# A decode step of attention and a small feed-forward: wo loaded as 24 and 8 rows a partition, and O placed by four matmuls

## The chip, the cores and the metric

The kernel runs on one core of one Trainium2 chip. The metric is the device time of one execution in microseconds (us): 343.64 us before the change, the median of three runs (343.55 to 343.87).

## The reference

One token for each of two sequences goes through attention over a cache of 4096 keys (32 heads of 128) and through a feed-forward layer with ReLU, and a sigmoid gate mixes the two. Cut to what matters:

```python
g = sigmoid((x * gate_w).sum(-1, keepdims=True))          # x: [2, 1, 512]
q = (x @ wq).reshape(2, 1, 32, 128).transpose(0, 2, 1, 3)
p = softmax(einsum("bhqd,bhkd->bhqk", q, k_cache) * 128 ** -0.5)
o = einsum("bhqk,bhkd->bhqd", p, v_cache)
a = o.transpose(0, 2, 1, 3).reshape(2, 1, 4096) @ wo       # wo: [4096, 512]
b = relu(x @ w1) @ w2                                      # w1: [512, 1376], w2: [1376, 512]
out = g * a + (1 - g) * b
```

All inputs are bf16. K and V are 67 MB each, wo is 4 MB, w2 1.4 MB; with wq and w1 145 MB are read once.

## The kernel before

**Memory.** K and V are cut into 8 units each (32,768 rows, 64 KB a partition). One tile `kv` of three regions (128 partitions x 3 x 64 KB) takes the units in turn, in an order written out by hand (`order`, line 164): K units 0 to 4, then V and K in turn, then V units 3 to 7. All transfers are issued by SP, in program order, and each waits only for PE to have finished with the unit that held its region three places earlier (`freed`). The last V unit comes in two transfers (48 rows of 64, then 16). Behind it, in the region that V unit 5 leaves, come w2 and wo.

**How the work is staged.** For a K unit DVE turns both halves in place (line 337), and PE accumulates scores for it (lines 342 and 370). After four K units the softmax of one sequence runs on DVE and ACT, and POOL spreads the probabilities into the weights `ptm` (line 408). For a V unit PE does 64 matmuls (line 425); ACT copies the sums out, POOL masks them, and a matmul gathers them (line 445). For the last V unit DVE does the masking (line 436).

**The tail.** After the last V unit PE's program order is: a few steps of w2 (`project_first`, lines 485 to 489: the rows of w2 in its first, small transfers), the gather of V unit 7, the other steps of w2's first part, `o_place`, then `project`. DVE scales O into `O_sb` (lines 459 and 461; 32 partitions, one for each head). `o_place` (line 465) brings O from heads on partitions to the layout in which it multiplies wo: 16 matmuls with shifted slices of a selection matrix `srow` (made once by POOL at line 253), into a PSUM area of 128 x 64, which ACT copies to `oW` (line 474). `project` (line 491) is 32 steps over wo and 9 over w2; one `step` (line 479) is two matmuls of 256 columns, side by side in two column groups of the array, for one row of wo or w2 a partition. A step that needs a new transfer waits for that transfer's semaphore, and everything behind it on PE waits too. At the end DVE and ACT cast the two halves of the sum (lines 502 and 504), and SP stores the output (line 244).

**The layout of wo and w2.** wo's 4096 rows lie as two halves of 2048; a partition holds 16 successive rows of each half. The three transfers are the first half (16 rows a partition, 16 KB), then 12 and 4 rows of the second (12 KB and 4 KB). `project` waits for them at steps 0, 16 and 28 (`lands`, line 492). w2's first 224 rows come in five small transfers ahead of wo; the other 1152 rows follow wo in blocks of 3, 3, 2 and 1 rows a partition (`W2`, line 210: semaphore, first row, rows a partition, first index). The hidden layer (`ffn_h`, line 308) is computed at the start, in the layout that w2's blocks ask for: for a block of n rows a partition, its weight loads take every n-th column of w1.

## Time and profile before

| | |
|---|---|
| median of three runs | 343.64 us |
| the profiled execution | 343.64 us |
| its span (first to last instruction) | 342.3 us |
| mean granted TensorE clock | 0.83 |
| PE busy | 190.9 us (56%) |
| DVE busy | 155.4 us (45%) |
| transfers of K, V and weights: share of the 16 DMA engines' time | 98.6% |
| read from HBM | 145.43 MB, 425 GB/s over the span |

The rows of a profile read as follows. A group or a timeline row names the engine, the line of the kernel, the operation, and what it writes and reads (`PS<-kv,oW` writes PSUM from the tiles kv and oW), with shape and count; in brackets stands how long the engine was idle ahead of it, and what ended that. PE is TensorE's matmuls, PEld its weight loads, which overlap matmuls. The chain of waits starts at the last instruction and goes back, at each step to what released it. The windows view gives, for chosen stretches, how long each engine was busy and, in brackets, how many instructions ran; PEclk is the clock that TensorE was granted, as a share of full speed. The granted clock is 1.00 or 0.50 in this kernel. A matmul's duration is longer than the distance to the next one, since they are pipelined.

### The profile page before, as it was taken

What the parts mean: (1) busy time and instruction counts of PE and PEld (TensorE: products, weight loads), DVE (VectorE), ACT (ScalarE), POOL (GpSimd) and SP (SyncE); (2) the same over time, 40 slices, a digit from 0 to 9 for tenths busy, and PEclk for the clock granted to TensorE, in tenths of its full rate; (3) what the DMA queues carried; (4) which work ended last, traced back from release to release, by engine and by line L of the source; (5) the groups of instructions that cost most, each with busy time, mean ns of one, the idle gap of its engine ahead of it and who ended that gap; (6) DMA issues with size and microseconds to landing.
All of it is one profiled execution on the core that took longest, in us unless ns stands there. A gap on an engine that the chain in (4) does not pass through costs nothing.

```text
span 342.3 us, 2418 instructions
## 1 busy us (share of the span) xinstructions
PE 190.9 (56%) x1294; PEld 40.1 (12%) x910; DVE 155.4 (45%) x41; ACT 13.1 (4%) x31; POOL 43.2 (13%) x55
## 2 busy tenths in 40 slices
PE   0520069595988909850992059900995532407386
PEld 0220001010000100010111001200012201102133
DVE  1000697979889779309900594009916000000010
ACT  1010000000000020000000000000003000000000
POOL 2000000000000004032005000050003250502300
PEclk9999999898798976995898559975799585857688
DMA  8998989899998989899999999898999999999996
GB/s 322 456 484 375 482 375 482 383 475 414 438 475 383 490 368 490 375 477 391 467 398 454 437 421 482 375 484 383 475 406 452 406 446 421 437 440 421 389 426 253
DMA packets 3810, 145.56 MB, mean 425 GB/s; under 512 B 445, under 2 KB 582, under 8 KB 1094
## 3 DMA queue, kind: packets, MB, share of 16 engines
q1 hardware_dynamic: 3796, 145.43, 98.6%
q8 instruction: 8, 0.13, 0.2%
q10 hardware_dynamic: 6, 0.00, 0.0%
HBM read 145.43 MB, written 0.00 MB: 425 GB/s over the span
## 4 chain that ended last, share of the span: by engine, by line
DMA 65%; PE 22%; DVE 10%; SPq 2%; issue 0%
DMA kv<-in_A_k_cache_dram 44%; PE PS L342 14%; DMA kv<-in_B_w_dram 11%; DVE kv L337 10%; DMA kv<-in_A_v_cache_dram 10%; PE PS L370 5%; PE PS L425 3%; SPq L231 1%; SPq L241 1%; SPq L236 0%; PE PS L481 0%; PE PS L445 0%; SPq L234 0%; SPq L216 0%; DVE ptm L502 0%
## 5 line engine op out<-in xcount | busy, mean ns | idle before, releaser
L337 DVE STREAM_TRANSPOSE kv<-kv 128x8192 uint32<-128x8192 uint32 x16 | 138.5, 8690 | 83.7 <-DMA kv<-in_A_k_cache_dram 83.7
L342 PE MATMUL PS<-kv,zero 128*128 128x512 bf16 x384 | 117.4, 417 | 0.0
L370 PE MATMUL PS<-kv,zero 128*128 128x512 bf16 x128 | 54.0, 422 | 93.8 <-DVE kv L337 84.6
L425 PE MATMUL PS<-kv,ptm 128*32 128x512 bf16 x512 | 39.4, 452 | 33.5 <-DMA kv<-in_A_v_cache_dram 33.5
L370 PEld LDWEIGHTS PS<-kv,zero 128*128 128x128 bf16 x128 | 13.3, 104 | 207.6 <-issue 112.3
L408 POOL TENSOR_TENSOR ptm<-E,mask 128x512 bf16<-128x512 bf16 x32 | 32.2, 1039 | 12.0 <-DVE E L399 11.1
L436 DVE TENSOR_TENSOR X<-PS,maskc 128x512 f32<-128x512 f32 x1 | 0.7, 692 | 62.7 <-PE PS L425 62.7
L425 PEld LDWEIGHTS PS<-kv,ptm 128*32 128x32 bf16 x512 | 16.1, 110 | 57.6 <-issue 48.2
L440 POOL TENSOR_TENSOR X<-X,maskc 128x512 f32<-128x512 f32 x7 | 7.3, 1038 | 114.3 <-ACT X L439 114.3
L330 POOL TENSOR_TENSOR zero<-q_sb,mask 128x32 bf16<-128x32 bf16 x8 | 2.0, 252 | 149.1 <-PE PS L342 133.6
L445 PE MATMUL PS<-X,zero 128*32 128x512 f32 x16 | 8.4, 604 | 6.8 <-POOL X L440 6.6
L439 ACT ACTIVATE X<-PS 128x512 f32<-128x512 f32 x7 | 4.2, 597 | 142.9 <-PE PS L425 142.9
L376 DVE TENSOR_REDUCE zero<-PS 128x2 f32<-128x2048 f32 x2 | 4.5, 2272 | 7.8 <-PE PS L342 7.8
L399 DVE STREAM_TRANSPOSE E<-E 128x2048 bf16<-128x2048 bf16 x2 | 4.6, 2311 | 4.7 <-ACT E L391 4.7
L294 PE MATMUL PS<-kv,zero 128*32 128x512 bf16 x32 | 3.6, 630 | 4.1 <-DMA kv<-in_A_wq_dram 4.1
L383 ACT ACTIVATE nrow<-mmax 128x32 f32<-128x32 f32 x2 | 0.5, 229 | 141.4 <-DVE mmax L380 141.4
L481 PE MATMUL PS<-kv,oW 128*2 128x256 bf16 x64 | 5.5, 344 | 0.7 <-DMA kv<-in_A_wo_dram 0.7
L272 PE MATMUL PS<-kv 3*128 3x3 bf16 x4 | 0.3, 166 | 8.1 <-DMA kv<-in_gate_w_dram 8.1
L502 DVE CAST ptm<-PS 2x256 bf16<-2x256 f32 x1 | 0.4, 412 | 9.3 <-PE PS L481 9.3
L301 DVE STREAM_TRANSPOSE ptm<-PS 128x1024 f32<-128x1024 f32 x1 | 1.2, 1249 | 7.2 <-PE PS L294 7.2
L391 ACT ACTIVATE E<-PS,negm 128x1024 bf16<-128x1024 f32 x4 | 4.4, 1110 | 0.6 <-DVE negm L387 0.6
L481 PE MATMUL PS<-kv,hT 20*2 20x256 bf16 (+2 forms) x42 | 3.2, 269 | 1.0 <-DMA kv<-in_B_w_dram 0.8
(43 smaller groups left out, 28.1 us busy)
## 6 DMA issues: line engine op xcount, KB each, us to landing
kv<-in_A_v_cache_dram SPq DMA_DIRECT2D x1, 6144.0 KB, 46.8
kv<-in_A_wq_dram SPq DMA_DIRECT2D x1, 4096.0 KB, 12.1
kv<-in_A_v_cache_dram SPq DMA_DIRECT2D x1, 2048.0 KB, 51.4
kv<-in_A_wo_dram SPq DMA_DIRECT2D x1, 2048.0 KB, 35.2
kv<-in_A_wo_dram SPq DMA_DIRECT2D x1, 1536.0 KB, 38.4
kv<-in_B_w_dram SPq DMA_DIRECT2D x1, 1376.0 KB, 15.0
kv<-in_B_w_dram SPq DMA_DIRECT2D x2, 384.0 KB, 40.0
kv<-in_A_wo_dram SPq DMA_DIRECT2D x1, 512.0 KB, 39.2
```

The costliest lines, as they stand in the source:

```text
L337: dve(lambda v, h=h: v.transpose(out=reg[:, 8192 * h:8192 * (h + 1)], in_=reg[:, 8192 * h:8192 * (h + 1)]), dwaits=([landed(what)] if h == ...
L342: return e.add_instruction(mybir.InstMatmult(name=nc.get_next_instruction_name(), engine=mybir.EngineType.PE, ins=[e.lower_ap(rhs), e.lowe ...
L370: return e.matmul(dst, lhsT=w, rhs=m, start=first, stop=final, skip_group_check=True)
L376: dve(lambda v: v.tensor_reduce(out=mpad[:, 0:2], in_=PSF[:, 0:2048].rearrange("p (x h q) -> p h x q", h=2, q=16), axis=AX.XY, op=ALU.max) ...
L391: act(lambda a, h=h: a.activation(out=E[:].rearrange("p (x h q) -> p h x q", h=2, q=16)[:, h], in_=PSF[:, 0:2048].rearrange("p (x h q) -> ...
L399: dve(lambda v: v.transpose(out=E[:], in_=E[:]), waits=[f"act_exp{b}"], signal=f"dve_et{b}")
L408: pool(lambda g, src=src, dst=dst: g.tensor_tensor(out=dst, in0=src, in1=msk, op=ALU.mult), waits=(([f"dve_et{b}"] if ub == 0 else []) + ( ...
L425: pe(lambda e, ci=ci, t=t: e.matmul(psf(32 * t, 32 * t + 32, c0, 512), lhsT=ptm[:, ci].rearrange("p c h -> p (c h)"), rhs=rows[:, 512 * ci ...
L439: act(lambda e: e.activation(out=X2[:], in_=src, func=ACT.Copy), waits=[f"pe_v_{v}"], signal=f"act_x_{v}")
L440: pool(lambda e: e.tensor_tensor(out=X, in0=X, in1=msk, op=ALU.mult), waits=[f"act_x_{v}"] + ([] if v else ["dve_setup"]), signal=f"pool_x ...
L445: pe(lambda e: e.matmul(psf(0, 32, O_C0, 512), lhsT=selx[:, 24 - 8 * ub:56 - 8 * ub], rhs=X2[:], start=(ub == 0), stop=(ub == 3), skip_gro ...
L481: pe(lambda e, g=g: e.matmul(psf(64 * g, 64 * g + 2, FIN_C0, 256), lhsT=w, rhs=m[:, 256 * g:256 * g + 256], start=start, stop=stop, tile_p ...
```

## The change

wo is laid out as 32 successive rows a partition and loaded in two transfers, of 24 and of 8 rows (24 KB and 8 KB a partition); `project` waits at steps 0 and 24. The order of wo's rows over partitions changes, and with it the placing of O: partition p now needs rows 32p to 32p + 31, a quarter of one head, so four matmuls of 64 columns do it, with one row of selection for each quarter, and `srow` shrinks from 263 to 131 columns. w2's two blocks of 3 rows become one of 6. The order of the steps on PE and of the transfers on SP stays as it was, and so do the bytes; two transfers and two semaphores go.

```diff
-    srow = zero[0:32, 788:920].bitcast(bf16)[:, 0:263]
+    srow = zero[0:32, 788:854].bitcast(bf16)[:, 0:131]
...
-    W2 = (("w2p", 0, 11, 0), ("w2p", 220, 1, 11), ("w2a", 224, 3, 12), ("w2b", 608, 3, 15), ("w2c", 992, 2, 18), ("w2d", 1248, 1, 20))
+    W2 = (("w2p", 0, 11, 0), ("w2p", 220, 1, 11), ("w2a", 224, 6, 12), ("w2c", 992, 2, 18), ("w2d", 1248, 1, 20))
...
-    for i, (x, r0, r1) in enumerate(((0, 0, 16), (1, 0, 12), (1, 12, 16))):
-        sp(lambda e, i=i, x=x, r0=r0, r1=r1: e.dma_start(
-            wo_sb[:, x * 8192 + r0 * 512:x * 8192 + r1 * 512],
-            A_wo[x * 2048:(x + 1) * 2048, :].rearrange("(p r) n -> p (r n)", p=128)[:, r0 * 512:r1 * 512])
+    for i, (a, b) in enumerate(((0, 24), (24, 32))):
+        sp(lambda e, i=i, a=a, b=b: e.dma_start(wo_sb[:, a * 512:b * 512], A_wo.rearrange("(p r) n -> p (r n)", r=32)[:, a * 512:b * 512])
            .then_inc(sem[f"wo{i}"], 16))
...
-        pool(lambda g: g.affine_select(out=srow, in_=srow, pattern=[[-1, 263]], compare_op=ALU.not_equal, fill=1.0,
-                                       base=7, channel_multiplier=8), waits=["c_zero"], signal="c_srow")
+        pool(lambda g: g.affine_select(out=srow, in_=srow, pattern=[[-1, 131]], compare_op=ALU.not_equal, fill=1.0,
+                                       base=3, channel_multiplier=4), waits=["c_zero"], signal="c_srow")
...
     def o_place():
-        for x in range(2):
-            for dq in range(8):
-                s0 = 128 * x - dq + 7
-                pe(lambda e, x=x, dq=dq, s0=s0: e.matmul(psf(0, 128, R_C0 + 32 * x, 32), lhsT=srow[:, s0:s0 + 128],
-                                                         rhs=O_sb[:, :, 16 * dq:16 * dq + 16], start=(dq == 0), stop=(dq == 7),
-                                                         tile_position=(0, 0), skip_group_check=True),
...
-        act(lambda a: a.activation(out=oW[:].rearrange("p (x r) c -> p x r c", x=2),
-                                   in_=psf(0, 128, R_C0, 64).rearrange("p (x b r) -> p x r b", x=2, b=2), func=ACT.Copy),
+        for dq in range(4):
+            pe(lambda e, dq=dq: e.matmul(psf(0, 128, R_C0, 64), lhsT=srow[:, 3 - dq:131 - dq],
+                                         rhs=O_sb[:, :, 32 * dq:32 * dq + 32], start=(dq == 0), stop=(dq == 3),
+                                         tile_position=(0, 0), skip_group_check=True),
+               waits=(["dve_O0", "dve_O1", "c_srow"] if dq == 0 else []), signal=("pe_R" if dq == 3 else None))
+        act(lambda a: a.activation(out=oW[:], in_=psf(0, 128, R_C0, 64).rearrange("p (b r) -> p r b", b=2), func=ACT.Copy),
             waits=["pe_R"], signal="act_oW")
...
     def project():
-        lands = {0: "wo0", 16: "wo1", 28: "wo2"}
+        lands = {0: "wo0", 24: "wo1"}
```

## The prediction

> **What bounds the kernel now.** I read the chain of waits first, then the timeline of the last 12 us, then the windows view with stretches cut where the granted clock changes. Until 327 us the page shows the DMA engines at 8 to 9 tenths in every slice, and the change touches nothing there that anybody waits for. What counts is the tail. The chain of waits ends so:

> ```profile
> 300.88 39.17 DMA kv<-in_B_w_dram
> 340.10 0.58 PE PS L481 x6
> 340.70 0.41 DVE ptm L502
> ```

> Columns: start, duration, what. The last w2 transfers land, six matmuls follow, then the cast. The end is set by a landing, and PE stands ready for it. The timeline shows how PE got there:

> ```profile
> 330.25 0.92 PE L481 MATMUL PS<-kv,hT 20*2 20x256 bf16 x14
> 331.47 0.56 PE L469 MATMUL PS<-zero 32*128 32x32 bf16 x16 [0.29 <-DVE zero L461]
> 332.07 0.22 ACT L474 ACTIVATE oW<-PS 128x64 bf16<-128x64 f32 x1 [17.67 <-PE PS L469]
> 332.69 5.47 PE L481 MATMUL PS<-kv,oW 128*2 128x256 bf16 x64 [0.66 <-DMA kv<-in_A_wo_dram]
> 336.24 1.62 PEld L481 LDWEIGHTS PS<-kv,oW 128*2 128x2 bf16 x32 [0.48 <-DMA kv<-in_A_wo_dram]
> 338.51 0.20 PEld L481 LDWEIGHTS PS<-kv,hT 128*2 128x2 bf16 x6 [0.65 <-DMA kv<-in_B_w_dram]
> 339.47 0.20 PEld L481 LDWEIGHTS PS<-kv,hT 128*2 128x2 bf16 x6 [0.76 <-DMA kv<-in_B_w_dram]
> 340.10 0.09 PEld L481 LDWEIGHTS PS<-kv,hT 128*2 128x2 bf16 x4 [0.43 <-DMA kv<-in_B_w_dram]
> 340.38 0.08 PEld L481 LDWEIGHTS PS<-kv,hT 128*2 128x2 bf16 x2 [0.20 <-DMA kv<-in_B_w_dram]
> 340.70 0.41 DVE L502 CAST ptm<-PS 2x256 bf16<-2x256 f32 x1 [9.29 <-PE PS L481]
> ```

> Each PEld row is PE released by a landing: the second wo transfer at 336.24, then w2a, w2b, w2c and w2d at 338.51, 339.47, 340.10 and 340.38. The first wo transfer released PE at 332.69. So a **step** (one row of wo or w2, two matmuls) is done while the next rows land.

> The third thing is the clock. In these rows the columns are the stretch, its length, PE busy (instructions), the other four engines, PEclk, DMA share, GB/s:

> ```profile
> 127.90:131.31 3.41, 2.46 (x6) 0.25 (x2) 2.57 (x2) 0.81 (x2) 0.18 (x1) 0.50 0.84 365
> 288.33:291.74 3.41, 2.99 (x32) 1.32 (x36) 0.00 (x0) 0.00 (x0) 0.00 (x0) 0.50 1.15 500
> 291.74:295.15 3.41, 2.10 (x40) 0.89 (x32) 0.00 (x0) 0.60 (x1) 0.58 (x1) 1.00 0.75 327
> 315.63:319.05 3.42, 0.98 (x2) 0.07 (x2) 0.00 (x0) 0.00 (x0) 3.42 (x4) 1.00 1.06 460
> 329.29:332.70 3.41, 2.46 (x34) 1.12 (x36) 1.01 (x2) 0.22 (x1) 0.00 (x0) 1.00 0.99 412
> 332.70:336.11 3.41, 3.41 (x32) 1.90 (x32) 0.00 (x0) 0.00 (x0) 0.00 (x0) 0.50 0.97 403
> 336.11:339.53 3.42, 2.60 (x42) 1.50 (x42) 0.00 (x0) 0.00 (x0) 0.00 (x0) 1.00 0.93 357
> ```

> The granted clock is 0.50 or 1.00 and changes only at steps of 3.41 us. A stretch at half clock was followed by full clock when PE was busy 2.99 us or more of it (288.33, 332.70), and by another half one at 2.46 us (127.90). A full stretch was followed by full at 2.10 us (291.74), by half at 0.98 us (315.63), and by half at 2.46 us where the work was 20- and 32-row matmuls (329.29).

> A step's price follows. At half clock, 16 steps fill 332.70 to 336.11: **0.213 us**. At full clock, the 14 matmuls from 330.25 are 7 steps in 0.92 us, of which the last matmul's own 0.27 is tail: 0.65 / 6 = **0.108 us**.

> **The change part by part.**

> O placed by 4 matmuls for 16. L469 took 0.56 us for 16, a start every 0.025 us. Four of 64 columns cost 4 x 0.025 at least and 4 x 0.054 (half a 256-column step) at most plus the 0.17 tail: 0.2 to 0.4 us saved, say 0.3. The cover: oW was ready at 332.29 and the first wo transfer released PE only at 332.69, and with the change PE waits for wo far longer, so this is worth 0. The smaller srow select (0.40 us on POOL at 2.5 us) is 325 us ahead of its use: 0.

> w2's stride in w1 goes from 3 to 6 columns for 24 of L314's weight loads (0.118 us each, at 16 to 19 us). No row shows the new stride; between nothing and a doubling it costs 0 to 2.8 us there. It holds up only the issue of the third K unit, whose turn on the DMA engines comes after two K units of about 20 us each (8.4 MB at the page's 425 GB/s): 0 either way.

> SP: two issues fewer (about 0.4 us each). SP issues all this from 297 to 321 us, 12 us and more ahead of the landings, and behind them only the output's issue stands, which waits for the cast: 0.

> DMA: the same bytes in 256 rows fewer and two transfers fewer. Rates between releases: 1.57 MB from 332.69 to 336.24 is 443 GB/s; 1.70 MB from 336.24 to 340.38 is 412. If all of the latter ran at 443 it would take 3.85 us for 4.14: at most 0.29 us gained. Only wo's last 4 rows and w2a, w2b get larger, so I take 0.1, with 0 and 0.29 as ends. That is the landing of w2d: 340.3.

> Now **the wait**. PE may start wo when 24 rows a partition have landed, not 16. The trace has landings at 16 rows (332.69) and 28 (336.24); two thirds between them is S = 332.69 + 8/12 x 3.55 = **335.05**. Ends: 332.69 and 336.24. Behind the wait stand all 41 remaining steps (32 of wo, 9 of w2), then both casts, then the output. PE's last work before it ends near 331.8, so it idles 3.2 us.

> At full clock the 41 steps would take 4.5 us, to 339.5, and PE would still be waiting for w2d. At half clock they take 8.7. Which one? With the profile's phase: 329.29 to 332.70 holds less work than before (L469 shrinks), and went to half even so. 332.70 to 336.11 then holds 1.06 us of PE work, under the 2.46 that did not suffice, so half goes on to 339.53. By then 4.48 / 0.213 = 21 steps are done; that stretch is full of work, so full clock follows. The last step begins 19 steps later: 339.53 + 19 x 0.108 = 341.60. From its start to the cast it was 340.38 to 340.70, 0.32 us: the cast starts at 341.92 instead of 340.70. **Sum: +1.2 us.** The w2 transfers are all in by 340.4, when PE is at about row 29 of wo: they are not waited for any more.

> The profiled execution took 343.64 us with a span of 342.3, the median of the three runs exactly, so 343.64 + 1.2 = **344.85**.

> The phase of the 3.41 us grid against the kernel need not be this one. If the clock doubles at B, the last step begins at S + 40 x 0.108 + (B - S)(1 - 0.108/0.213), and B - S lies between about 2.7 (a stretch just busy enough) and 2.7 + 3.41: casts from +0.35 to +2.0, so 344.0 to 345.65, with the profile's +1.2 in the middle. With S at its late end, 336.24, it is +1.8; at its early end nothing, since the landings would hide it.

> [...]

> **The rivals.**

> A (14%): the clock stays at full over the wait. Then PE does its 41 steps by 339.6 and w2d's landing sets the end: 343.64 less 0 to 0.29, **343.5**, not slower. It decides if PE idling under one stretch of 3.41 us isn't enough to halve the clock, or if S is under about 333.6, so that 332.70 to 336.11 is busy enough. Against it: 329.29 to 332.70 halved the clock with PE busy for 2.46 us. [...]

> B (3%): joining transfers is worth more than the rates show, and PE keeps up. If each of the two boundaries removed costs what a whole small transfer took (w2d, 340.10 to 340.38: 0.28 us), 0.56 goes, and with the 0.29 above 0.85: 342.8. Against it: the transfers follow one another at 404 to 468 GB/s. [...]

> C (4%): the clock never returns to full in the tail: 335.05 + 40 x 0.213 + 0.32 = 343.9 for the cast, +3.2: **346.8**. Each full stretch of half clock in the trace was followed by full, which speaks against it.

> D (3%): the change doesn't delay PE, because 24 rows land together with what was 16 (all engines fetch both ends in parallel): 343.5.

> **How the numbers follow.** The forecast, half clock from S for one and a bit stretches, has 76%: 344.85. About 0.2% (0.69 us) is what a measurement of this kernel tells from no change: 342.95 to 344.33 is "same". Of the forecast's phases the lowest sixth falls under 344.33, 12%. Same: A 14, D 3 and that 12: 29%. Faster: B, 3%. Slower: the forecast's other 64 and C's 4, 68%. The range runs from A's 343.5 to 345.5, leaving out the latest phases, B and C.

> **What would show it.** PE's first wo matmul near 335.0, released by the wo DMA; PEclk 0.50 from about 332.7 past 336; no PE idle time before the w2 matmuls; the cast near 341.9. Runs of the changed kernel should scatter by up to 1.6 us, where those of before lie within 0.3. Wrong would be: full clock at 336 with PE waiting for w2d at 340.3 (A), or S near 333 (D).

## The result, and the profile after

The changed kernel takes 344.89 us, the median of 18 runs, for 343.79 before (18 runs); the ratio is 1.0029, 95% interval 1.0021 to 1.0037. That is 1.1 us slower. The runs of before lie from 343.55 to 344.5; those of the changed kernel from 343.94 to 345.54, in two groups: six from 343.94 to 344.29, twelve from 344.73 to 345.54. The profile shown is of the quickest of them (343.94 us, span 342.6), which must be kept in mind when it is read.

The chain of waits of the changed kernel now ends with 41 steps of PE without a break (82 matmuls, of which the chain names 78), and the landing that releases them is wo's, not w2's:

```profile
298.21 36.67 DMA kv<-in_A_wo_dram
334.88 0.14 issue
335.02 5.95 PE PS L475 x78
...
340.99 0.41 DVE ptm L496
```

The timeline of the changed kernel, same columns as before (L465 places O, L469 copies it, L475 is the step):

```profile
331.66 0.29 PE L465 MATMUL PS<-zero 32*128 32x64 bf16 x4 [0.28 <-DVE zero L459]
331.99 0.22 ACT L469 ACTIVATE oW<-PS 128x64 bf16<-128x64 f32 x1 [16.76 <-PE PS L465]
335.02 4.94 PE L475 MATMUL PS<-kv,oW 128*2 128x256 bf16 x64 [3.07 <-DMA kv<-in_A_wo_dram]
339.79 1.15 PE L475 MATMUL PS<-kv,hT 128*2 128x256 bf16 x18
340.99 0.41 DVE L496 CAST ptm<-PS 2x256 bf16<-2x256 f32 x1 [9.38 <-PE PS L475]
```

PE idles 3.07 us until 24 rows of wo have landed, and the row of w2's 18 matmuls has no bracket: PE waits for no transfer of w2 any more. The windows view, cut where the granted clock changes (the last three columns are PEclk, DMA share, GB/s):

```profile
330.86:334.27 3.41, 0.80 (x14) 0.33 (x8) 0.71 (x2) 0.22 (x1) 0.00 (x0) 1.00 0.89 372
334.27:337.68 3.41, 2.66 (x26) 1.71 (x28) 0.00 (x0) 0.00 (x0) 0.00 (x0) 0.50 1.00 414
337.68:341.10 3.42, 3.26 (x60) 2.31 (x54) 0.12 (x1) 0.12 (x1) 0.00 (x0) 1.00 0.43 167
```

In this run the 3.41 us grid lies 1.6 us later, counted from the first instruction, than in the profile of before. The wait falls into 330.86 to 334.27, PE is busy for 0.80 us of it, and the clock is halved at 334.27, just before PE starts at 335.02. The next stretch, with 2.66 us of work, is followed by full clock at 337.68: the luckiest phase the forecast named.

### The profile page after: what moved, and what is told of

Read it like the earlier page. It is cut to its first block, busy times and chain, and to the rows that moved or that the text cites. A ratio compares the mean times of both kernels' runs of the same rounds, so it can differ in the third digit from the quotient of the medians.

```text
span 342.6 us, 2392 instructions
## 1 busy us (share of the span) xinstructions
PE 190.5 (56%) x1282; PEld 41.0 (12%) x898; DVE 154.7 (45%) x41; ACT 13.1 (4%) x31; POOL 43.1 (13%) x55
## 4 chain that ended last, share of the span: by engine, by line
DMA 64%; PE 21%; DVE 13%; SPq 1%; issue 0%
DMA kv<-in_A_k_cache_dram 43%; DVE kv L335 13%; PE PS L340 12%; DMA kv<-in_A_wo_dram 11%; DMA kv<-in_A_v_cache_dram 10%; PE PS L368 4%; PE PS L423 3%; PE PS L475 2%; SPq L231 1%; PE PS L443 0%; SPq L234 0%; DVE ptm L496 0%; SPq L216 0%; SPq L215 0%
## 5 line engine op out<-in xcount | busy, mean ns | idle before, releaser
L340 PE MATMUL PS<-kv,zero 128*128 128x512 bf16 x384 | 116.2, 413 | 0.0
L368 PE MATMUL PS<-kv,zero 128*128 128x512 bf16 x128 | 53.5, 418 | 93.8 <-DVE kv L335 85.2
L423 PE MATMUL PS<-kv,ptm 128*32 128x512 bf16 x512 | 40.5, 464 | 32.6 <-DMA kv<-in_A_v_cache_dram 32.6
L475 PE MATMUL PS<-kv,oW 128*2 128x256 bf16 x64 | 4.9, 329 | 3.1 <-DMA kv<-in_A_wo_dram 3.1
L475 PEld LDWEIGHTS PS<-kv,oW 128*2 128x2 bf16 x64 | 3.3, 100 | 4.6 <-issue 3.2
```

The source lines that it names most:

```text
L340: return e.add_instruction(mybir.InstMatmult(name=nc.get_next_instruction_name(), engine=mybir.EngineType.PE, ins=[e.lower_ap(rhs), e.lowe ...
L368: return e.matmul(dst, lhsT=w, rhs=m, start=first, stop=final, skip_group_check=True)
L423: pe(lambda e, ci=ci, t=t: e.matmul(psf(32 * t, 32 * t + 32, c0, 512), lhsT=ptm[:, ci].rearrange("p c h -> p (c h)"), rhs=rows[:, 512 * ci ...
L475: pe(lambda e, g=g: e.matmul(psf(64 * g, 64 * g + 2, FIN_C0, 256), lhsT=w, rhs=m[:, 256 * g:256 * g + 256], start=start, stop=stop, tile_p ...
```

## The experiments

The theory: PE starts wo 2.3 us later, and after a wait long enough that the clock is halved. The steps at half price cost more than the slack that PE had at the end. Rivals: W, w2's six rows behind one landing make PE late; L, the new layout or the larger transfers land later; and that the late start costs by itself, whatever the clock.

**The wait undone, all else kept** (label wo_16_12_4; the list of semaphores, which gets `wo2` back, is left out here).

```diff
-    for i, (a, b) in enumerate(((0, 24), (24, 32))):
+    for i, (a, b) in enumerate(((0, 16), (16, 28), (28, 32))):
...
-        lands = {0: "wo0", 24: "wo1"}
+        lands = {0: "wo0", 16: "wo1", 28: "wo2"}
```

> The changed kernel with wo in three transfers of 16, 12 and 4 rows again, waited for at steps 0, 16 and 28; layout, four placing matmuls and w2's block of six stay. Theory (the 24-row wait starts PE late and cold): PE starts wo at 332.7 as before, the landing of w2d sets the end again, so 343.5 to 343.8 us and runs within about 0.5 us of each other. Rival W (w2's six rows behind one landing make PE late): still about 344.9. Rival L (the new layout with rows 32 KB apart loads slower): still above 344.3.

Measured: 343.68 us (343.47 to 344.3, 11 runs), ratio to before 0.9997 (0.9988 to 1.0005). The loss is gone, with the new layout, the four placing matmuls and the block of six in place. W falls, and of L the layout; that transfers as large as the changed kernel's need not cost shows below, in warm, which keeps them.

**A still later start** (label wo_28_4).

```diff
-    for i, (a, b) in enumerate(((0, 24), (24, 32))):
+    for i, (a, b) in enumerate(((0, 28), (28, 32))):
...
-        lands = {0: "wo0", 24: "wo1"}
+        lands = {0: "wo0", 28: "wo1"}
```

> The changed kernel with wo in transfers of 28 and 4 rows, waited for at steps 0 and 28: as many transfers as in the changed kernel, but PE starts at about 336.2 instead of 335.0. Theory: the cast starts at S + 4.36 + 0.49 x (B - S) + 0.32 with S = 336.2 and B - S between 2.7 and 6.1, so 342.2 to 343.9 for 340.7 before: 345.3 to 347.0 us, median near 346.1. Rivals W and L, and any by which the size or number of transfers is the cost: no change from the changed kernel, 344.9.

Measured: 345.78 us (345.12 to 346.84, 6 runs), ratio 1.0056 (1.0041 to 1.0071); the median is 0.3 below the expected one, the quickest run 0.2 below the range. As many transfers as in the changed kernel, and twice the loss. Its profile is of the slowest run, and the windows show the unlucky phase:

```profile
331.96:335.37 3.41, 0.29 (x4) 0.17 (x4) 0.19 (x1) 0.22 (x1) 0.00 (x0) 1.00 0.92 389
335.37:338.79 3.42, 2.41 (x24) 1.55 (x26) 0.00 (x0) 0.00 (x0) 0.00 (x0) 0.50 0.96 388
338.79:342.20 3.41, 3.41 (x36) 2.12 (x34) 0.00 (x0) 0.00 (x0) 0.00 (x0) 0.50 0.18 67
```

PE started at 336.38 and was busy for 2.41 us of the second stretch. The stretch behind it still went at half clock from end to end, while the DMA engines had almost nothing left to do (share 0.18).

**The wait alone, put into the kernel before** (label late_start).

```diff
-    for i, (x, r0, r1) in enumerate(((0, 0, 16), (1, 0, 12), (1, 12, 16))):
+    for i, (x, r0, r1) in enumerate(((0, 0, 16), (1, 0, 8), (1, 8, 16))):
...
-        lands = {0: "wo0", 16: "wo1", 28: "wo2"}
+        lands = {0: ("wo0", "wo1"), 24: ("wo2",)}
...
-                 dwaits=([(sem[lands[r]], 16)] if r in lands else []))
+                 dwaits=[(sem[s], 16) for s in lands.get(r, ())])
```

> The kernel before with nothing of the change but the wait: wo in its old layout in three transfers of 16, 8 and 8 rows, PE waits for the first two (24 rows) at step 0; 16 placing matmuls, w2 in blocks of 3, 3, 2 and 1. Theory: the whole loss comes with the wait, so about 344.9 us with runs from 343.9 to 345.6. Rivals W and L: as before, 343.8 us, runs within about 0.5.

Measured: 344.76 us (344.1 to 345.8, 10 runs), ratio 1.0024 (1.0011 to 1.0036). Old layout, 16 placing matmuls, as many transfers as before (wo's second and third are of 8 and 8 rows for 12 and 4): the wait brings the loss and the scatter.

```profile
335.22 5.32 PE L481 MATMUL PS<-kv,oW 128*2 128x256 bf16 x64 [2.51 <-DMA kv<-in_A_wo_dram]
340.38 1.15 PE L481 MATMUL PS<-kv,hT 128*2 128x256 bf16 x18
341.57 0.41 DVE L502 CAST ptm<-PS 2x256 bf16<-2x256 f32 x1 [9.48 <-PE PS L481]
```

This is its timeline: 2.51 us of idle time, then all steps without a wait, as in the changed kernel. In its windows the clock is halved just behind PE's start at 335.22 and doubles at 338.76:

```profile
335.35:338.76 3.41, 3.41 (x36) 2.23 (x34) 0.00 (x0) 0.00 (x0) 0.00 (x0) 0.50 0.95 378
338.76:342.18 3.42, 2.77 (x50) 2.03 (x46) 0.41 (x1) 0.38 (x1) 0.00 (x0) 1.00 0.21 78
```

**The late start with the clock kept up** (label warm). Eight matmuls, whose result nothing reads, are added to the changed kernel inside the wait.

```diff
     o_place()
+    for i in range(8):
+        pe(lambda e: e.matmul(psf(0, 128, V_C0, 512), lhsT=E[:, 0:128], rhs=E[:, 0:512], start=True, stop=True,
+                              skip_group_check=True), waits=(["act_x_6"] if i == 0 else []))
     project()
```

> The changed kernel with 8 added matmuls of 512 columns between the placing of O and the steps over wo, into a PSUM bank that nothing reads any more: 1.7 us of PE at full clock, 3.4 at half, in a wait of 3.1. Theory: with PE busy through most of the wait the clock is at full when wo lands or soon after, PE catches up, and w2d's landing sets the end in most runs: 343.5 to 343.9 us median, single runs up to 344.3. A rival by which the late start itself costs, whatever the clock (41 steps behind one landing): 344.9 or more, since work is added.

Measured: 343.6 us (343.48 to 343.78, 11 runs), ratio to before 0.9993 (0.9984 to 1.0001). Work added, 1.3 us gained on the changed kernel, and the scatter gone. In the windows of this run the wait falls into the first row:

```profile
332.61:336.02 3.41, 1.80 (x23) 0.96 (x22) 0.00 (x0) 0.00 (x0) 0.00 (x0) 1.00 0.90 380
336.02:339.44 3.42, 2.80 (x54) 2.07 (x50) 0.00 (x0) 0.00 (x0) 0.00 (x0) 1.00 0.90 359
```

and its timeline has PE starting wo as late as in the changed kernel, yet waiting for w2 again:

```profile
335.12 3.66 PE L475 MATMUL PS<-kv,oW 128*2 128x256 bf16 x64 [1.61 <-DMA kv<-in_A_wo_dram]
339.40 1.22 PE L475 MATMUL PS<-kv,hT 128*2 128x256 bf16 x18 [0.62 <-DMA kv<-in_B_w_dram]
340.34 0.08 PEld L475 LDWEIGHTS PS<-kv,hT 128*2 128x2 bf16 x2 [0.20 <-DMA kv<-in_B_w_dram]
```

The 32 steps of wo took 3.66 us where the changed kernel took 4.94, and the landings of w2 set the end again (w2a's at 339.40, w2d's at 340.34). So a start at 335.1 costs nothing by itself, and neither do the larger transfers: the clock is the cost.

**The same for 28 and 4 rows** (label warm_28_4): the edit of wo_28_4, and 12 of the added matmuls.

> Transfers of 28 and 4 rows, with 12 added matmuls of 512 columns in the wait for the first (2.6 us at full clock, 5.1 at half, in a wait of 3.9). Theory: started at 336.3 with the clock at full, the 41 steps end near 340.7 and the cast starts near 340.9: 343.8 to 344.2 us, where the same transfers without the added work took 345.8. Rival (the late start is the cost, not the clock): 345.8 or more.

Measured: 344.0 us (343.76 to 345.94, 11 runs), ratio 1.0009 (0.9998 to 1.002). Ten of the runs are at or below 344.21, for 345.12 to 346.84 without the added work. Its profile casts at 341.05 for 340.66 in warm: here PE never waits for w2, so all 41 steps, even at full clock (4.66 us from PE's start at 336.37), just fail to fit. What that costs is too small for the interval, which includes 1. One run took 345.94: the twelve added matmuls were expected to take 5.1 us at half clock, more than the wait of 3.9 (an estimate; in the profile, at full clock, eleven of them on record took 2.54 us), and would then hold up wo. But there is no profile of that run, so its cause stays open.

**A shorter wait** (label wo_20_12).

```diff
-    for i, (a, b) in enumerate(((0, 24), (24, 32))):
+    for i, (a, b) in enumerate(((0, 20), (20, 32))):
...
-        lands = {0: "wo0", 24: "wo1"}
+        lands = {0: "wo0", 20: "wo1"}
```

> The changed kernel with wo in transfers of 20 and 12 rows: PE starts at about 333.9. Theory: the cast would start at S + 4.36 + 0.49 x (B - S) + 0.32 with B - S from 2.7 to 6.1, so 339.9 to 341.5, but not ahead of w2d's landing, 340.7: about half of the runs as before, 343.6 to 343.8, the others up to 344.5; median 343.7 to 344.1. A rival by which two transfers of any split cost the same: 344.9.

Measured: 343.58 us (343.4 to 343.91, 11 runs), ratio 0.9994 (0.9985 to 1.0003). That there is no loss left at the median fits, though the median lies 0.1 us below the expected range; that no run went over 343.91, where half were to reach up to 344.5, does not fit. The windows of its slowest run show one reason:

```profile
331.34:334.75 3.41, 1.35 (x26) 0.83 (x22) 0.69 (x2) 0.22 (x1) 0.00 (x0) 1.00 0.93 387
334.75:338.16 3.41, 3.41 (x38) 2.10 (x34) 0.00 (x0) 0.00 (x0) 0.00 (x0) 0.50 0.98 407
```

PE started at 334.18, while the clock still stood at full, and lost it only at 334.75. The formula has half clock from the start in every phase, which overstates the cost of a short wait. Whether that alone accounts for all eleven runs is not shown.

**w2's block of six alone** (label w2_block; the list of semaphores, which loses `w2b`, is left out here).

```diff
-    W2 = (("w2p", 0, 11, 0), ("w2p", 220, 1, 11), ("w2a", 224, 3, 12), ("w2b", 608, 3, 15), ("w2c", 992, 2, 18), ("w2d", 1248, 1, 20))
+    W2 = (("w2p", 0, 11, 0), ("w2p", 220, 1, 11), ("w2a", 224, 6, 12), ("w2c", 992, 2, 18), ("w2d", 1248, 1, 20))
```

> The kernel before with w2's block of six rows alone (one transfer and 128 rows fewer). Theory: PE stands ready for w2 at 338.2, does the 6 steps in 0.65 us after a landing near 339.4, and w2d's landing sets the end: within 0.2 us of before, 343.5 to 343.8. Rival W (six rows behind one landing make PE late): 344.0 or more. Rival J (joined transfers save what a transfer boundary costs): 343.3 or less.

Measured: 343.75 us (343.51 to 344.33, 11 runs), ratio 1.0001 (0.9992 to 1.001): nothing, either way. Its timeline has PE released at 339.54 by w2a and ready again for w2c and w2d:

```profile
339.54 1.25 PE L481 MATMUL PS<-kv,hT 128*2 128x256 bf16 x18 [1.25 <-DMA kv<-in_B_w_dram]
340.23 0.09 PEld L481 LDWEIGHTS PS<-kv,hT 128*2 128x2 bf16 x4 [0.17 <-DMA kv<-in_B_w_dram]
340.51 0.08 PEld L481 LDWEIGHTS PS<-kv,hT 128*2 128x2 bf16 x2 [0.19 <-DMA kv<-in_B_w_dram]
```

Of all these kernels none is faster than before beyond its interval; warm and wo_20_12 (343.6) come nearest, and both beat the changed kernel.

## Why the prediction was right

The forecast was 344.85 us and the measured median is 344.89. The mechanism is the one forecast. That the numbers meet within 0.04 us is partly luck: the sum was worked out for one phase of the grid, and the runs spread over 1.6 us. By its own steps:

- **The start of wo.** Forecast 335.05 from the landings at 16 and 28 rows; measured 335.02 in the one profile. Profiles differ by more than that: PE's first w2 steps begin at 328.41 in the profile of before and at 328.61 in this one.
- **The price of a step and the sum.** The forecast's formula puts the cast at S + 40 x 0.108 + (B - S) x 0.493 + 0.32 (the expectations round the step up to 0.109, so 4.36 stands there). With each profile's own S and B it can be checked without the phase:

| kernel | PE starts (S) | clock doubles (B) | cast by the formula | cast measured |
|---|---|---|---|---|
| changed | 335.02 | 337.68 | 340.97 | 340.99 |
| late_start | 335.22 | 338.76 | 341.61 | 341.57 |
| wo_28_4 | 336.38 | 342.20 | 343.89 | 343.89 |

In the forecast's own sum, 339.53 + 19 x 0.108 is 341.58 and not 341.60; the +1.2 us stays.

- **The phase.** Forecast: runs scattered over 344.0 to 345.65; measured 343.94 to 345.54. The runs of before lay within 0.95 us, not within the 0.3 that the forecast took from three runs. The phase did change from profile to profile: the grid stands at 334.27 in one, 335.37 in another. Runs without a profile have a mean granted clock on record, and their times go with it. Of the changed kernel's eighteen, the five with 0.826 to 0.841 are neighbours in time (344.29 to 344.99 us); all five quicker ones have 0.781, and the eight slower ones (345.10 to 345.54) 0.777 to 0.796. In late_start the four with 0.826 to 0.841 are neighbours in the middle as well (344.51 to 345.02); in warm, with values from 0.786 to 0.85, no such order shows (343.48 to 343.78). This fits a phase that changes from run to run and sets the time. The forecast put the lowest sixth of its phases under 344.33 us (evenly spread, 0.33 of its 1.65 us is a fifth); a third of the runs (6 of 18) lie there.
- **Rival A, the clock survives the wait.** It did not: half clock followed a stretch with 0.80 us of PE work, and in wo_20_12 one with 1.35 us. The trace of before had shown the like (0.98 us from 315.63, 2.46 us from 329.29). One reading of that trace was incomplete. The forecast calls the work from 329.29 20- and 32-row matmuls, but 1.04 of its 2.46 us are the gather, with 128 rows:

```profile
329.28 1.04 PE L445 MATMUL PS<-X,zero 128*32 128x512 f32 x2 [0.16 <-DVE X L436]
```

- **Rivals C and D.** The clock did return to full in the tail, at 337.68, and 24 rows landed at 335.02, not with what was 16.
- **The placing of O.** Forecast 0.3 us saved and worth 0; measured 0.56 to 0.29 on PE, ahead of a wait of 3 us. (The forecast's bounds for the four matmuls give 0.2 to 0.3 us saved, not 0.2 to 0.4.)
- **Joined transfers.** Forecast 0.1 us earlier for w2d's landing, from 0 to 0.29. Neither w2_block (1.0001) nor wo_16_12_4 (0.9997) shows it; their intervals allow 0.3 and 0.4 us. The two transfers joined in w2_block are of 384 KB each, and its runs show no gain.
- **The stride of w1's weight loads.** Forecast 0 to 2.8 us at that place and 0 for the kernel; L312's matmuls end 0.5 us later than before (last start 19.7 for 19.2 us), and wo_16_12_4, which has it, loses nothing.

What stays open: whether the phase is evenly spread over runs (two groups of times and a third of low runs rather leave that in doubt; in the nine profiles the edges near 332 us lie between 330.86 and 332.73, within 1.9 of the 3.41 us), why no run of wo_20_12 was long, and the one long run of warm_28_4.

## What to carry to other kernels

Where the last transfers of a kernel feed matmuls as they land, do not join them so that TensorE waits much longer and then has all the work behind it. Here the wait of 3.07 us for 24 rows was followed by a granted clock of 0.50 (to 337.68), and the 41 steps behind it took 5.95 us, where the same steps took 4.66 at full clock (warm_28_4): the slack was gone. How much longer matters: here a wait for 20 rows (PE idle for 1.77 us) cost nothing, and for 24 it cost 1.1 us. Work out the tail at both clocks (here 0.213 and 0.108 us a step), and from the number of steps still to do when the transfer lands. If a longer wait is unavoidable, matmuls that nobody needs can be cheaper than idling: here eight of them in the wait gave 343.6 us for 344.89.

## What the runs showed of the hardware

| clock of the stretch | PE busy where full clock followed | PE busy where half clock followed |
|---|---|---|
| 0.50 | 2.66 us (changed kernel, from 334.27) or more, 25 stretches | 2.46 us (before, from 127.90) or less, 53 stretches |
| 1.00 | 1.59 us (before, from 312.22; changed kernel, from 293.31 and 313.79) or more, 75 stretches | 1.46 us (before, from 261.02) or less, 23 stretches, and two busier ones |

The stretches of the other runs' tails that stand above lie on the same sides: behind half clock, 2.41 us in wo_28_4 was followed by half and 3.41 by full; behind full clock, 1.80 us in warm was followed by full, 0.29 in wo_28_4 and 1.35 in wo_20_12 by half. So 1.80 us of work was seen to keep the full clock, while 2.41 us at half clock was seen not to bring it back. Where between the values of a row the outcome changes, and whether it does so at the same place in every run, is not shown.

The two busier ones hold small matmuls. In the changed kernel's trace the stretch from 16.83 us, whose 79 matmuls are the hidden layer's, of 2 columns each, was busy for 3.07 us, and half clock followed. In before the stretch from 329.29 was busy for 2.46 us, with matmuls of 20 and 32 rows beside 1.04 us of the gather; so was one in wo_16_12_4, from 329.31, for 2.51 us, and half clock followed both. Whether the kind of matmul is the reason was not tried.
